# Another opening for a gated attention and SwiGLU kernel: first x tile ahead of the loads, split copies, held transposes, fixed PSUM banks

## The chip, the cores and the metric

The kernel runs on one core of a Trainium2 chip. Its time is device microseconds of one execution; lower is better. The program was executed three times before the change, with a median of 181.58 us (180.75 to 183.9). One further execution was taken with the hardware profiler; durations in this text come from it.

## The reference: what is computed

The input x has 2048 tokens of 512 features, in bf16. Two branches are computed and mixed by a gate per token:

```python
g = sigmoid((x * gate_w).sum(-1, keepdims=True))
qkv = x @ wqkv                      # 32 heads of 16
pq, pk = phi(q), phi(k)             # phi(t) = where(t>0, t+1, exp(t)) + 1e-6
kv  = einsum("bhsd,bhse->bhde", pk, v);  z = pk.sum(over tokens)
a = (pq @ kv / (pq @ z + 1e-6)) @ wo
b = (silu(x @ w1) * (x @ w3)) @ w2  # hidden size 1376
out = g * a + (1 - g) * b
```

The attention is linear: no score matrix exists, and kv is a 16 by 16 matrix per head.

## The kernel before

Tokens are cut into 16 tiles of 128 (index t) and four blocks of 512; the 512 features into four chunks of 128 (index kc). The order of the work on each engine is written out by hand: the program's order of calls is the order of instructions, and semaphore waits between engines are put in from the data that each instruction reads and writes. A PSUM tile taken from a pool waits for the last reader of the buffer that it gets.

TensorE needs x twice: token-major (xN, loaded as it is) and feature-major (xT). For the first four tiles xT is made on the chip: transpose_step (L195 to L201) transposes four 128x128 pieces of xN on TensorE into one bf16 PSUM tile, and VectorE copies all 512 columns into xT (L201). For the other twelve tiles xT comes by transposing DMAs from DRAM (L97, L100): four of 512 tokens by 128 features, then four of 1024 by 128.

All loads are issued at the top from two queues, that of SyncE (SP) and that of ScalarE (ACT). Eight DMA semaphores are used in turn: the ninth DMA of the program, the load of wq, waits for the landing of the first, and so on.

The stages on TensorE are these. The opening: ten matmuls on zeros (warm, L205), transposition of tile 0, two more warm matmuls, half of the k projection of tile 0, transposition of tile 1, the other half, transposition of tile 2, k of tile 1, transposition of tile 3, k of tiles 2 and 3. Then a loop over the tiles: the q projection of tile t, the k projection of tile t+2, and g_step, which accumulates x^T pk for tile t in four PSUM banks. phi is an Exp on ScalarE (L165) and two VectorE operations (L167, L170); each k tile is added to zacc on GpSimd (POOL, L184). After the loop come the small products for kv and its product with wo, and for each block of 512 tokens ten gate and up pairs (L251, L257), the remainder of the hidden size (rem_step), and four output steps (L378, L392).

For the prediction the order in which VectorE and ScalarE get the opening matters. Before the change all four copies of L201 stand on VectorE ahead of the first phi, because the two calls of k_phi come after the last transpose_step:

```python
transpose_step(2, psumT)
k1 = project(1, wk, "k")
transpose_step(3, psumT)
k_phi(0, k0)
k_phi(1, k1)
```

Of the kernel before, what the change touches and what calls it, by code (L numbers as in the profile page):

```python
# [16 lines left out]
def kernel(  # L17
# [17 lines left out]
    nc = tc.nc  # L35
# [12 lines left out]
    FR = F - FC * P  # L48
    F0 = FC * P
    HPC = P // Dh  # L50
    NR = 2 * FR + 1
    NPE = TPB
    ZP = 4

    x2d = A_x.flatten_outer_dims()
    out2d = out.flatten_outer_dims()
    x_r = x2d.rearrange("s (kc d) -> s kc d", d=P)
    x_t = x2d.rearrange("(t p) d -> p t d", p=P)
    wqkv_r = A_wqkv.rearrange("(kc d) n -> d kc n", d=P)
    w1_r = B_w1.rearrange("(kc d) f -> d kc f", d=P)  # L60
# [1 line left out]

    consts = ctx.enter_context(tc.tile_pool(name="consts", bufs=1))
    work = ctx.enter_context(tc.tile_pool(name="work", bufs=2))
    psum = ctx.enter_context(tc.tile_pool(name="psum", bufs=4, space=bass.MemoryType.PSUM))
    ctx.enter_context(tc.manual_schedule())

    warm = consts.tile([P, 256], BF16, name="warm")
    nc.vector.memset(warm[:], 0.0)
    ident = consts.tile([P, P], BF16, name="ident")  # L70
    make_identity(nc, ident[:])

# [8 lines left out]
    w3 = consts.tile([P, KC, F0], BF16, name="w3")  # L81
    w2 = consts.tile([P, FC + 1, D], BF16, name="w2")
    xT = consts.tile([P, KC, S], BF16, name="xT")
    dq = nc.sync
    aq = nc.scalar
    k_cols = slice(D, 2 * D)
    dq.dma_start(out=xN[:, 0, :], in_=x_t[:, 0, :])
    aq.dma_start(out=wk[:, 0, :], in_=wqkv_r[:, 0, k_cols])
    dq.dma_start(out=wk[:, 1, :], in_=wqkv_r[:, 1, k_cols])
    aq.dma_start(out=xN[:, 1, :], in_=x_t[:, 1, :])  # L90
    dq.dma_start(out=wk[:, 2, :], in_=wqkv_r[:, 2, k_cols])
    aq.dma_start(out=wk[:, 3, :], in_=wqkv_r[:, 3, k_cols])
    dq.dma_start(out=xN[:, 2, :], in_=x_t[:, 2, :])
    aq.dma_start(out=xN[:, 3, :], in_=x_t[:, 3, :])
    dq.dma_start(out=wq[:], in_=wqkv_r[:, :, 0:D])
    for kc in range(KC):
        dq.dma_start(out=xT[:, kc, TB : 2 * TB], in_=x_r[TB : 2 * TB, kc, :], transpose=True)  # L97
    dq.dma_start(out=xN[:, 4:8, :], in_=x_t[:, 4:8, :])
    for kc in range(KC):
        dq.dma_start(out=xT[:, kc, 2 * TB : S], in_=x_r[2 * TB : S, kc, :], transpose=True)  # L100
    dq.dma_start(out=xN[:, 8:12, :], in_=x_t[:, 8:12, :])
    dq.dma_start(out=xN[:, 12:16, :], in_=x_t[:, 12:16, :])
    with nc.allow_non_contiguous_dma(reason="gate column"):
        dq.dma_start(
            out=wr[:, :, 2 * FR : NR], in_=gate_w.rearrange("(kc d o) -> d kc o", d=P, o=1)
# [41 lines left out]
    def mm_tile(name):
        return psum.tile([P, D], FP32, tag="mm", name=name)


    def project(t, w, name, between=None):
        ts = slice(t * P, (t + 1) * P)
        ps = mm_tile(name + "_ps")
        for kc in range(KC):
            nc.tensor.matmul(  # L155
                ps[:], lhsT=xT[:, kc, ts], rhs=w[:, kc, :],
                start=(kc == 0), stop=(kc == KC - 1),
            )
            if kc == 1 and between is not None:
                between()  # L160
        return ps
# [25 lines left out]
                )  # L187

    def k_step(t):
        k_phi(t, project(t, wk, "k"))  # L190

    def q_step(t):
        phi(project(t, wq, "q"), pq[:, t, :], "q")

    def transpose_step(t, pool):  # L195
        ps = pool.tile([P, KC, P], BF16, tag="xTp", name="xTp")
        for kc in range(KC):
            nc.tensor.transpose(  # L198
                out=ps[:, kc, :], in_=xN[:, t, kc * P : (kc + 1) * P], identity=ident[:]
            )  # L200
        nc.vector.tensor_copy(out=xT[:, :, t * P : (t + 1) * P], in_=ps[:])  # L201

    def warm_step(ps, n):
        for _ in range(n):
            nc.tensor.matmul(  # L205
                ps[:, 0:256], lhsT=warm[:, 0:P], rhs=warm[:], start=True, stop=True
            )


    def rem_step(tb):  # L210

        hr = hrem[tb % 2]
        for half in range(2):
            ps = psum.tile([P, 2, 256], FP32, tag="mm", name="r_ps")
            for j in range(2):
                t = tb * TPB + half * 2 + j
# [28 lines left out]

    def glu_step(tb, fc):
        fs = slice(fc * P, (fc + 1) * P)
        tok = slice(tb * TB, (tb + 1) * TB)
        g_ps = mm_tile("gate_ps")
        for kc in range(KC):  # L250
            nc.tensor.matmul(  # L251
                g_ps[:], lhsT=w1[:, kc, fs], rhs=xT[:, kc, tok],
                start=(kc == 0), stop=(kc == KC - 1),
            )
        u_ps = mm_tile("up_ps")
        for kc in range(KC):
            nc.tensor.matmul(  # L257
                u_ps[:], lhsT=w3[:, kc, fs], rhs=xT[:, kc, tok],
# [40 lines left out]

    hT = {}  # L300
    hT[0] = work.tile([P, FC + 1, TB], BF16, tag="hT", name="hT")
    with tc.tile_pool(name="psumT", bufs=NPE, space=bass.MemoryType.PSUM) as psumT:
        w_ps = mm_tile("warm_ps")
        warm_step(w_ps, 10)
        transpose_step(0, psumT)
        warm_step(w_ps, 2)
        k0 = project(0, wk, "k", between=lambda: transpose_step(1, psumT))
        transpose_step(2, psumT)
        k1 = project(1, wk, "k")
        transpose_step(3, psumT)  # L310
        k_phi(0, k0)
        k_phi(1, k1)
    with tc.tile_pool(name="psumG", bufs=KC, space=bass.MemoryType.PSUM) as psumG:
        g_acc = [psumG.tile([P, D], FP32, tag="G", name=f"g_acc{kc}") for kc in range(KC)]

        def g_step(t):
            for kc in range(KC):
# [5 lines left out]
        k_step(2)
        k_step(3)
        q_step(0)
        g_step(0)
        q_step(1)
        g_step(1)
        for t in range(2, NT):
            q_step(t)  # L330
            if t + 2 < NT:
                k_step(t + 2)
            g_step(t)
        z_ps = mm_tile("z_ps")
        nc.tensor.matmul(z_ps[:], lhsT=ones[:], rhs=zaccb[:], start=True, stop=True)  # L335
        nc.vector.tensor_copy(out=zb[:], in_=z_ps[:])  # L336
        for kc in range(KC):
            if kc % 2 == 0:
                nc.vector.tensor_copy(out=Gsb[:, kc, :], in_=g_acc[kc][:])
            else:  # L340
                nc.scalar.activation(out=Gsb[:, kc, :], in_=g_acc[kc][:], func=ACT.Copy)

    psum2 = ctx.enter_context(tc.tile_pool(name="psum2", bufs=4, space=bass.MemoryType.PSUM))

    def ab_tile(name):
        return psum2.tile([P, D], FP32, tag="ab", name=name)

    def kv_step():
        kv_ps = psum2.tile([P, KC, P], FP32, tag="ab", name="kv_ps")
        for c in range(KC):  # L350
            cs = slice(c * P, (c + 1) * P)
            for kc in range(KC):
# [2 lines left out]
                    start=(kc == 0), stop=(kc == KC - 1),  # L355
                )
        nc.vector.tensor_tensor(
            out=kvT[:], in0=kv_ps[:],
            in1=bmask[:].rearrange("p h d -> p (h d)")[:, None, :].to_broadcast([P, KC, P]),
            op=ALU.mult,  # L360
        )

    def m2_step():
        for c in range(KC):
            ps = ab_tile("m2_ps")
            nc.tensor.matmul(ps[:], lhsT=kvT[:, c, :], rhs=wo[:, c, :], start=True, stop=True)  # L366
            if c % 2 == 0:
                nc.scalar.activation(out=M2[:, c, :], in_=ps[:], func=ACT.Copy)
# [3 lines left out]
    def out_step(tb, tt):  # L372
        t = tb * TPB + tt
        ts = slice(t * P, (t + 1) * P)
        tl = slice(tt * P, (tt + 1) * P)
        a_ps = ab_tile("a_ps")
        for c in range(KC):
            nc.tensor.matmul(  # L378
                a_ps[:], lhsT=pqT[:, c, ts], rhs=M2[:, c, :],
# [6 lines left out]
        w = D // pieces  # L386
        for i in range(pieces):
            cs = slice(i * w, (i + 1) * w)
            b_ps = ab_tile("b_ps")
            for fc in range(FC + 1):  # L390
                n = P if fc < FC else FR
                nc.tensor.matmul(  # L392
# [61 lines left out]
```

## Time and profile before

| what | value |
|---|---|
| time, median of three executions | 181.58 us (180.75 to 183.9) |
| time of the profiled execution | 181.63 us |
| its span, first to last instruction | 179.6 us |
| TensorE busy | 174.3 us, 97% |
| VectorE, ScalarE, GpSimd busy | 101.4, 61.8, 62.8 us |
| TensorE busy from 0 to 3.59 us, from 3.59 to 7.25, from 7.25 to 10.11 | 2.32, 3.57, 2.86 us |
| bytes moved by DMA | 14.88 MB |

The span leaves out what lies around the instructions: 181.63 - 179.6 = 2.03 us. TensorE's busy time is a sum of instruction records; matmuls overlap and their ends are modelled, so 97% says that it hardly ever stands still, not that it runs at its peak. A row of a timeline gives the start, the length, the engine and source line, the output and inputs, and in brackets how long the engine was idle ahead of it and what released it. SPq and ACTq are the queues' sequencers that issue DMAs. Landing times are counted from the issue of a DMA to its semaphore.

### The profile page before, as it was taken

To read this page: it belongs to the slowest core of one execution; us is meant where nothing else is said; L and a number is where in the kernel's file an instruction comes from. 1 tells how busy PE (TensorE), PEld (TensorE's weight loads), DVE (VectorE), ACT (ScalarE), POOL (GpSimd) and SP (SyncE) were. 2 spreads that over 40 slices of the span, in tenths; PEclk is the share of its full clock that TensorE was granted. 3 is DMA by queue.
4 is the path that set the end of the run, shared out by engine and by line. 5 is a ranking of instruction groups with operands and counts; after the bars stand their busy time and mean duration, and the time that the engine had idled before them with its cause. 6 is when DMAs were issued, how large, how long until landed. Compare 5 with 4: busy or idle time off the path is not lost.

```text
span 179.6 us, 2468 instructions
## 1 busy us (share of the span) xinstructions
PE 174.3 (97%) x860; PEld 84.4 (47%) x876; DVE 101.4 (56%) x196; ACT 61.8 (34%) x110; POOL 62.8 (35%) x105
## 2 busy tenths in 40 slices
PE   7999999999999999999999999999999999999993
PEld 4544444444445464544444454444445544444452
DVE  0398898888799672566343355644335564433222
ACT  2254454445562442222323212232321323332130
POOL 5066565676477440445400044540004432000000
PEclk9999999999999999999999999999999999999999
DMA  5989999910002112033200003520000342000011
GB/s 166 248 217 206 256 306 401 378 55 5 0 0 53 35 28 34 29 88 88 58 0 4 0 29 88 89 62 0 0 0 29 89 91 59 0 0 0 29 44 48
DMA packets 28108, 14.88 MB, mean 83 GB/s; under 512 B 19424, under 2 KB 27072, under 8 KB 28096
## 3 DMA queue, kind: packets, MB, share of 16 engines
q1 hardware_dynamic: 27520, 14.20, 30.1%
q10 hardware_dynamic: 576, 0.52, 0.8%
q8 instruction: 7, 0.11, 0.3%
q14 instruction: 5, 0.04, 0.1%
HBM read 8.42 MB, written 2.10 MB: 59 GB/s over the span
## 4 chain that ended last, share of the span: by engine, by line
PE 96%; DMA 2%; issue 1%; DVE 1%
PE b_ps L392 21%; PE gate_ps L251 19%; PE up_ps L257 19%; PE k_ps L155 8%; PE g_acc L318 8%; PE a_ps L378 8%; PE q_ps L155 8%; PE r_ps L218 3%; DMA xN<-in_A_x_dram 2%; PE xTp L198 1%; PE kv_ps L353 0%; PE m_ps L366 0%; DVE o L396 0%; DVE xT L201 0%; PE z_ps L335 0%
## 5 line engine op out<-in xcount | busy, mean ns | idle before, releaser
L263 DVE TENSOR_TENSOR hT<-up_ps,sg 128x512 bf16<-128x512 f32 x40 | 27.2, 680 | 31.0 <-PE up_ps L257 27.8
L251 PE MATMUL gate_ps<-xT,w 128*128 128x512 bf16 x158 | 41.0, 379 | 0.3
L392 PE MATMUL b_ps<-w,hT 128*128 128x512 bf16 (+3 forms) x186 | 40.6, 367 | 0.1
L257 PE MATMUL up_ps<-xT,w 128*128 128x512 bf16 x154 | 40.3, 379 | 0.2
L262 ACT ACTIVATE sg<-gate_ps 128x512 bf16<-128x512 f32 x40 | 23.9, 597 | 46.9 <-PE gate_ps L251 46.9
L285 POOL TENSOR_TENSOR pqs<-pq,rden 128x512 bf16<-128x512 bf16 x16 | 16.9, 1056 | 65.0 <-issue 60.0
L396 DVE SCALAR_TENSOR_TENSOR o<-b_ps,omg_all,aga 128x512 bf16<-128x512 f32 (+1 forms) x17 | 12.2, 720 | 28.3 <-PE b_ps L392 28.3
L392 PEld LDWEIGHTS <-hT 128*128 128x128 bf16 (+1 forms) x187 | 18.3, 98 | 19.9
L184 POOL TENSOR_TENSOR zacc<-zacc,pk 128x128 f32<-128x128 f32 x56 | 23.1, 444 | 11.5 <-DVE pk L170 11.5
L257 PEld LDWEIGHTS <-w 128*128 128x128 bf16 x160 | 15.7, 98 | 18.9
L251 PEld LDWEIGHTS <-w 128*128 128x128 bf16 x160 | 15.6, 98 | 18.5
L383 ACT ACTIVATE aga<-a_ps,g_all 128x512 f32<-128x512 f32 x16 | 11.0, 687 | 28.9 <-PE a_ps L378 28.9
L155 PEld LDWEIGHTS <-xT 128*128 128x128 bf16 x128 | 12.5, 100 | 14.7 <-DVE xT L201 0.6
L270 POOL TENSOR_TENSOR pr<-pq,zb 128x512 f32<-128x512 bf16 x16 | 18.4, 1156 | 1.7 <-DVE zb L336 1.7
L155 PE MATMUL k_ps<-wk,xT 128*128 128x512 bf16 x62 | 17.1, 396 | 0.2
L318 PE MATMUL g_acc<-pk,xN 128*128 128x512 bf16 x63 | 16.4, 379 | 0.1
L378 PE MATMUL a_ps<-M,pqT 128*128 128x512 bf16 x61 | 16.3, 378 | 0.2
L155 PE MATMUL q_ps<-wq,xT 128*128 128x512 bf16 x63 | 16.2, 379 | 0.0
L165 ACT ACTIVATE eq<-q_ps 128x512 bf16<-128x512 f32 x16 | 9.6, 597 | 17.2 <-PE q_ps L155 16.1
L165 ACT ACTIVATE ek<-k_ps 128x512 bf16<-128x512 f32 x16 | 9.6, 597 | 7.7 <-PE k_ps L155 7.5
L170 DVE SCALAR_TENSOR_TENSOR pk<-k_ps,emk 128x512 bf16<-128x512 f32 x16 | 11.1, 692 | 1.6
L170 DVE SCALAR_TENSOR_TENSOR pq<-q_ps,emq 128x512 bf16<-128x512 f32 x16 | 11.1, 692 | 0.5
(47 smaller groups left out, 94.7 us busy)
## 6 DMA issues: line engine op xcount, KB each, us to landing
w<-in_B_w_dram SPq DMA_DIRECT2D x3, 1280.0 KB, 8.5
out_dram<-o SPq DMA_DIRECT2D x15, 128.0 KB, 1.9
xN<-in_A_x_dram SPq DMA_DIRECT2D x3, 512.0 KB, 6.1
wq<-in_A_wqkv_dram SPq DMA_DIRECT2D x1, 512.0 KB, 4.7
wv<-in_A_wqkv_dram SPq DMA_DIRECT2D x1, 512.0 KB, 9.0
wo<-in_A_wo_dram SPq DMA_DIRECT2D x1, 512.0 KB, 9.5
wk<-in_A_wqkv_dram ACTq DMA_DIRECT2D x2, 128.0 KB, 3.4
xN<-in_A_x_dram SPq DMA_DIRECT2D x2, 128.0 KB, 3.3
```

Of the source, the lines that this page charges most:

```text
L155: nc.tensor.matmul(ps[:], lhsT=xT[:, kc, ts], rhs=w[:, kc, :], start=(kc == 0), stop=(kc == KC - 1),)
L165: nc.scalar.activation(out=e[:], in_=ps[:], func=ACT.Exp)
L170: nc.vector.scalar_tensor_tensor(out=dst, in0=ps[:], scalar=0.0, in1=em[:], op0=ALU.max, op1=ALU.add)
L184: nc.gpsimd.tensor_tensor(out=(zaccb if t == NT - 1 else zacc)[:, cs], in0=zacc[:, cs], in1=pk[t][:, cs], op=ALU.add,)
L251: nc.tensor.matmul(g_ps[:], lhsT=w1[:, kc, fs], rhs=xT[:, kc, tok], start=(kc == 0), stop=(kc == KC - 1),)
L257: nc.tensor.matmul(u_ps[:], lhsT=w3[:, kc, fs], rhs=xT[:, kc, tok], start=(kc == 0), stop=(kc == KC - 1),)
L262: nc.scalar.activation(out=sg[:], in_=g_ps[:], func=ACT.Silu)
L263: nc.vector.tensor_tensor(out=hT[tb][:, fc, :], in0=u_ps[:], in1=sg[:], op=ALU.mult)
L270: nc.gpsimd.tensor_tensor(out=pr[t][:], in0=pq[:, t, :], in1=zb[:], op=ALU.mult)
L318: nc.tensor.matmul(g_acc[kc][:], lhsT=xN[:, t, kc * P : (kc + 1) * P], rhs=pk[t][:], start=(t == 0), stop=(t == NT - 1),)
L378: nc.tensor.matmul(a_ps[:], lhsT=pqT[:, c, ts], rhs=M2[:, c, :], start=(c == 0), stop=(c == KC - 1),)
L392: nc.tensor.matmul(b_ps[:, 0:w], lhsT=hT[tb][:n, fc, tl], rhs=w2[:n, fc, cs], start=(fc == 0), stop=(fc == FC),)
```

## The change

Six things differ; the arithmetic of everything after the opening is the same, in the same order on TensorE.

1. **Loads.** SP issues x tile 0, wk chunks 0 and 2, x tiles 2 and 3, then wq in two halves. ACT first runs a one-element Exp (which brings the load of its function table with it) and then issues wk chunks 1 and 3 and x tile 1. Before, ACT issued wk 0, x tile 1, wk 3 and x tile 3 before any other work, and SP x tile 0, wk 1, wk 2, x tile 2 and wq in one piece.
2. **Warm matmuls** read a constant of ones that exists before the program's first barrier, in place of a tile of zeros written by VectorE. Three stand after tile 0's transposition in place of two.
3. **Transposes of tiles 0 to 3** are plain matmuls with the identity into two fp32 banks, two pieces each; VectorE copies one half (256 columns), ScalarE the other.
4. **The order of the copies and phi**: phi of tile 0 is called before the transposition of tile 3, and phi of tile 1 after it.
5. **Transposing DMAs**: twelve, one per tile of 128 tokens by 512 features. GpSimd writes one column of xT from the first half of wq; the first transposing DMA overwrites it and so waits for that half.
6. **PSUM**: eight fixed banks that are used in turn (0 to 3 for transposes, the g sums, kv, M2 and the output; 4 to 7 for projections, gate, up and remainder), in place of pools that are opened and closed.

```diff
-    warm = consts.tile([P, 256], BF16, name="warm")
-    nc.vector.memset(warm[:], 0.0)
+    warm = nc.const_aps.tensor(1.0, [P, 256], BF16)
...
-    dq.dma_start(out=xN[:, 0, :], in_=x_t[:, 0, :])
-    aq.dma_start(out=wk[:, 0, :], in_=wqkv_r[:, 0, k_cols])
-    dq.dma_start(out=wk[:, 1, :], in_=wqkv_r[:, 1, k_cols])
-    aq.dma_start(out=xN[:, 1, :], in_=x_t[:, 1, :])
-    dq.dma_start(out=wk[:, 2, :], in_=wqkv_r[:, 2, k_cols])
-    aq.dma_start(out=wk[:, 3, :], in_=wqkv_r[:, 3, k_cols])
-    dq.dma_start(out=xN[:, 2, :], in_=x_t[:, 2, :])
-    aq.dma_start(out=xN[:, 3, :], in_=x_t[:, 3, :])
-    dq.dma_start(out=wq[:], in_=wqkv_r[:, :, 0:D])
-    for kc in range(KC):
-        dq.dma_start(out=xT[:, kc, TB : 2 * TB], in_=x_r[TB : 2 * TB, kc, :], transpose=True)
-    dq.dma_start(out=xN[:, 4:8, :], in_=x_t[:, 4:8, :])
-    for kc in range(KC):
-        dq.dma_start(out=xT[:, kc, 2 * TB : S], in_=x_r[2 * TB : S, kc, :], transpose=True)
-    dq.dma_start(out=xN[:, 8:12, :], in_=x_t[:, 8:12, :])
-    dq.dma_start(out=xN[:, 12:16, :], in_=x_t[:, 12:16, :])
+    def load_xT(t):
+        ts = slice(t * P, (t + 1) * P)
+        dq.dma_start(out=xT[:, :, ts], in_=x2d[ts, :], transpose=True)
...
+    load_xN(dq, 0, 1)
+    nc.scalar.activation(out=act_pre[:], in_=warm[:, 0:1], func=ACT.Exp)
+    load_wk(dq, 0)
+    load_wk(aq, 1)
+    load_wk(dq, 2)
+    load_wk(aq, 3)
+    load_xN(aq, 1, 2)
+    load_xN(dq, 2, 3)
+    load_xN(dq, 3, 4)
+    for h in range(2):
+        hs = slice(2 * h, 2 * h + 2)
+        dq.dma_start(out=wq[:, hs, :], in_=wqkv_r[:, hs, 0:D])
+
+    nc.gpsimd.tensor_copy(out=xT[:, 0, TB : TB + 1], in_=wq[:, 1, 0:1])
+    for t in range(TPB, NT):
+        load_xT(t)
+        if t in (5, 7, 11):
+            i = {5: 4, 7: 8, 11: 12}[t]
+            load_xN(dq, i, i + 4)
...
+    bank = [psum.tile([P, D], FP32, name=f"bank{i}") for i in range(8)]
+    turn = {"mm": 0, "ab": 0}
+
+    def mm_tile():
+        turn["mm"] += 1
+        return bank[4 + (turn["mm"] - 1) % 4]
+
+    def ab_tile():
+        turn["ab"] += 1
+        return bank[(turn["ab"] - 1) % 4]
...
-        warm_step(w_ps, 10)
-        transpose_step(0, psumT)
-        warm_step(w_ps, 2)
-        k0 = project(0, wk, "k", between=lambda: transpose_step(1, psumT))
-        transpose_step(2, psumT)
-        k1 = project(1, wk, "k")
-        transpose_step(3, psumT)
-        k_phi(0, k0)
-        k_phi(1, k1)
+    def transpose_step(t, lo, hi):
+
+        ts = slice(t * P, (t + 1) * P)
+        for ps, k0 in ((lo, 0), (hi, 2)):
+            for kc in (k0, k0 + 1):
                 nc.tensor.matmul(
+                    ps[:, (kc - k0) * P : (kc - k0 + 1) * P],
+                    lhsT=xN[:, t, kc * P : (kc + 1) * P], rhs=ident[:],
+                    start=True, stop=True,
                 )
+        half = [p[:, 0 : 2 * P].rearrange("p (kc q) -> p kc q", q=P) for p in (lo, hi)]
+        nc.vector.tensor_copy(out=xT[:, 0:2, ts], in_=half[0])
+        nc.scalar.activation(out=xT[:, 2:4, ts], in_=half[1], func=ACT.Copy)
+
+    warm_step(10)
+    transpose_step(0, bank[0], bank[1])
+    warm_step(3)
+    k0 = project(0, wk, between=lambda: transpose_step(1, bank[0], bank[1]))
+    transpose_step(2, bank[2], bank[3])
+    k_phi(0, k0)
+    k1 = project(1, wk)
+    transpose_step(3, bank[0], bank[1])
+    k_phi(1, k1)
+    k_step(2)
+    k_step(3)
```

More of the change, by code (lines that the diff above doesn't have):

```diff
@@ L50 @@
     HPC = P // Dh
+    ZP = 4
     NR = 2 * FR + 1
-    NPE = TPB
-    ZP = 4
     x2d = A_x.flatten_outer_dims()
     out2d = out.flatten_outer_dims()
-    x_r = x2d.rearrange("s (kc d) -> s kc d", d=P)
     x_t = x2d.rearrange("(t p) d -> p t d", p=P)
@@ L64 @@
     work = ctx.enter_context(tc.tile_pool(name="work", bufs=2))
-    psum = ctx.enter_context(tc.tile_pool(name="psum", bufs=4, space=bass.MemoryType.PSUM))
+    psum = ctx.enter_context(tc.tile_pool(name="psum", bufs=1, space=bass.MemoryType.PSUM))
     ctx.enter_context(tc.manual_schedule())
-    warm = consts.tile([P, 256], BF16, name="warm")
-    nc.vector.memset(warm[:], 0.0)
+    warm = nc.const_aps.tensor(1.0, [P, 256], BF16)
     ident = consts.tile([P, P], BF16, name="ident")
@@ L83 @@
     xT = consts.tile([P, KC, S], BF16, name="xT")
+    act_pre = consts.tile([P, 1], BF16, name="act_pre")
     dq = nc.sync
@@ L86, with load_xN, load_wk @@
     k_cols = slice(D, 2 * D)
-    dq.dma_start(out=xN[:, 0, :], in_=x_t[:, 0, :])
-    aq.dma_start(out=wk[:, 0, :], in_=wqkv_r[:, 0, k_cols])
-    dq.dma_start(out=wk[:, 1, :], in_=wqkv_r[:, 1, k_cols])
-    aq.dma_start(out=xN[:, 1, :], in_=x_t[:, 1, :])
-    dq.dma_start(out=wk[:, 2, :], in_=wqkv_r[:, 2, k_cols])
-    aq.dma_start(out=wk[:, 3, :], in_=wqkv_r[:, 3, k_cols])
-    dq.dma_start(out=xN[:, 2, :], in_=x_t[:, 2, :])
-    aq.dma_start(out=xN[:, 3, :], in_=x_t[:, 3, :])
-    dq.dma_start(out=wq[:], in_=wqkv_r[:, :, 0:D])
-    for kc in range(KC):
-        dq.dma_start(out=xT[:, kc, TB : 2 * TB], in_=x_r[TB : 2 * TB, kc, :], transpose=True)
-    dq.dma_start(out=xN[:, 4:8, :], in_=x_t[:, 4:8, :])
-    for kc in range(KC):
-        dq.dma_start(out=xT[:, kc, 2 * TB : S], in_=x_r[2 * TB : S, kc, :], transpose=True)
-    dq.dma_start(out=xN[:, 8:12, :], in_=x_t[:, 8:12, :])
-    dq.dma_start(out=xN[:, 12:16, :], in_=x_t[:, 12:16, :])
+    def load_xT(t):
+        ts = slice(t * P, (t + 1) * P)
+        dq.dma_start(out=xT[:, :, ts], in_=x2d[ts, :], transpose=True)
+    def load_xN(q, t0, t1):
+        q.dma_start(out=xN[:, t0:t1, :], in_=x_t[:, t0:t1, :])
+    def load_wk(q, kc):
+        q.dma_start(out=wk[:, kc, :], in_=wqkv_r[:, kc, k_cols])
+    load_xN(dq, 0, 1)
[16 more added lines that the diff above has]
+            load_xN(dq, i, i + 4)
     with nc.allow_non_contiguous_dma(reason="gate column"):
@@ L145, with project @@
     th_all = consts.tile([P, NT], FP32, name="th_all")
[L147 to L153, printed above, removed]
+    bank = [psum.tile([P, D], FP32, name=f"bank{i}") for i in range(8)]
[6 more added lines that the diff above has]
+        return bank[(turn["ab"] - 1) % 4]
+    def project(t, w, between=None):
+        ps = mm_tile()
         for kc in range(KC):
             nc.tensor.matmul(
-                ps[:], lhsT=xT[:, kc, ts], rhs=w[:, kc, :],
+                ps[:], lhsT=xT[:, kc, t * P : (t + 1) * P], rhs=w[:, kc, :],
                 start=(kc == 0), stop=(kc == KC - 1),
@@ L189, in k_step, with g_step @@
     def k_step(t):
-        k_phi(t, project(t, wk, "k"))
+        k_phi(t, project(t, wk))
     def q_step(t):
-        phi(project(t, wq, "q"), pq[:, t, :], "q")
-    def transpose_step(t, pool):
-        ps = pool.tile([P, KC, P], BF16, tag="xTp", name="xTp")
+        phi(project(t, wq), pq[:, t, :], "q")
+    def g_step(t):
         for kc in range(KC):
[L198 to L204, printed above, removed]
             nc.tensor.matmul(
-                ps[:, 0:256], lhsT=warm[:, 0:P], rhs=warm[:], start=True, stop=True
+                bank[kc][:], lhsT=xN[:, t, kc * P : (kc + 1) * P], rhs=pk[t][:],
+                start=(t == 0), stop=(t == NT - 1),
             )
@@ L213, in rem_step @@
         for half in range(2):
-            ps = psum.tile([P, 2, 256], FP32, tag="mm", name="r_ps")
+            ps = mm_tile()[:].rearrange("p (j n) -> p j n", j=2)
             for j in range(2):
@@ L248, in glu_step @@
         tok = slice(tb * TB, (tb + 1) * TB)
-        g_ps = mm_tile("gate_ps")
+        g_ps = mm_tile()
         for kc in range(KC):
@@ L254, in glu_step @@
             )
-        u_ps = mm_tile("up_ps")
+        u_ps = mm_tile()
         for kc in range(KC):
@@ L301 @@
     hT[0] = work.tile([P, FC + 1, TB], BF16, tag="hT", name="hT")
-    with tc.tile_pool(name="psumT", bufs=NPE, space=bass.MemoryType.PSUM) as psumT:
-        w_ps = mm_tile("warm_ps")
-        warm_step(w_ps, 10)
-        transpose_step(0, psumT)
-        warm_step(w_ps, 2)
-        k0 = project(0, wk, "k", between=lambda: transpose_step(1, psumT))
-        transpose_step(2, psumT)
-        k1 = project(1, wk, "k")
-        transpose_step(3, psumT)
-        k_phi(0, k0)
-        k_phi(1, k1)
@@ L313, with warm_step @@
[L313 to L317, printed above, removed]
+    def warm_step(n):
+        for _ in range(n):
+            nc.tensor.matmul(
+                bank[3][:, 0:256], lhsT=warm[:, 0:P], rhs=warm, start=True, stop=True
+            )
+    def transpose_step(t, lo, hi):
+        ts = slice(t * P, (t + 1) * P)
+        for ps, k0 in ((lo, 0), (hi, 2)):
+            for kc in (k0, k0 + 1):
@@ L318, in g_step @@
                 nc.tensor.matmul(
-                    g_acc[kc][:], lhsT=xN[:, t, kc * P : (kc + 1) * P], rhs=pk[t][:],
-                    start=(t == 0), stop=(t == NT - 1),
-                )
[L323 to L346, printed above, removed]
+                    ps[:, (kc - k0) * P : (kc - k0 + 1) * P],
@@ new lines @@
+    transpose_step(2, bank[2], bank[3])
[5 more added lines that the diff above has]
+    k_step(3)
+    q_step(0)
+    g_step(0)
+    q_step(1)
+    g_step(1)
+    for t in range(2, NT):
+        q_step(t)
+        if t + 2 < NT:
+            k_step(t + 2)
+        g_step(t)
+    z_ps = mm_tile()
+    nc.tensor.matmul(z_ps[:], lhsT=ones[:], rhs=zaccb[:], start=True, stop=True)
+    nc.vector.tensor_copy(out=zb[:], in_=z_ps[:])
@@ L348, in kv_step @@
+    for kc in range(KC):
+        if kc % 2 == 0:
+            nc.vector.tensor_copy(out=Gsb[:, kc, :], in_=bank[kc][:])
+        else:
+            nc.scalar.activation(out=Gsb[:, kc, :], in_=bank[kc][:], func=ACT.Copy)
     def kv_step():
-        kv_ps = psum2.tile([P, KC, P], FP32, tag="ab", name="kv_ps")
+        kv_ps = ab_tile()[:].rearrange("p (c q) -> p c q", q=P)
         for c in range(KC):
@@ L357, in kv_step @@
         nc.vector.tensor_tensor(
-            out=kvT[:], in0=kv_ps[:],
+            out=kvT[:], in0=kv_ps,
             in1=bmask[:].rearrange("p h d -> p (h d)")[:, None, :].to_broadcast([P, KC, P]),
@@ L364, in m2_step @@
         for c in range(KC):
-            ps = ab_tile("m2_ps")
+            ps = ab_tile()
             nc.tensor.matmul(ps[:], lhsT=kvT[:, c, :], rhs=wo[:, c, :], start=True, stop=True)
@@ L375, in out_step @@
         tl = slice(tt * P, (tt + 1) * P)
-        a_ps = ab_tile("a_ps")
+        a_ps = ab_tile()
         for c in range(KC):
@@ L388, in out_step @@
             cs = slice(i * w, (i + 1) * w)
-            b_ps = ab_tile("b_ps")
+            b_ps = ab_tile()
             for fc in range(FC + 1):
```

## The prediction, made before the changed kernel ran

> **What bounds the kernel now.** I read the page's totals and its chain of waits first.
>
> ```profile
> span 179.6 us, 2468 instructions
> PE 174.3 (97%) x860; PEld 84.4 (47%) x876; DVE 101.4 (56%) x196; ACT 61.8 (34%) x110; POOL 62.8 (35%) x105
> ...
> PE 96%; DMA 2%; issue 1%; DVE 1%
> ```
>
> The chain that ended last lies 96% on TensorE, and the 2% of DMA is one transfer: x tile 0. From the opening on TensorE does not stand still, so an edit counts by how much earlier or later it lets the stream of matmuls run. Next I read the chain for the first microseconds (start, length, what).
>
> ```profile
> 0.80 2.74 DMA xN<-in_A_x_dram
> ...
> 4.71 1.03 PE k_ps L155 x2
> 5.75 0.43 PE xTp L198 x4
> 6.17 0.85 PE k_ps L155 x2
> 7.03 0.43 PE xTp L198 x4
> 7.45 0.87 PE k_ps L155 x4
> 8.32 0.22 PE xTp L198 x4
> 8.55 1.73 PE k_ps L155 x8
> ```
>
> Two k matmuls take 0.85 us at 6.17, four take 0.87 from 7.45: TensorE runs at half pace until about 7.3 us, although its clock column is full throughout. By matmul starts in the timeline the second transposition begins at 5.54, the third at 6.82, k of tile 1 at 7.25, k of tile 2 at 8.38 and k of tile 3 at 8.38 + 0.865 = 9.24. From there the stream is unbroken, so the start of **k of tile 3** after the change, against 9.24, is nearly the whole answer. The timeline shows what feeds it.
>
> ```profile
> 2.70 1.28 ACT L165 ACT_TABLE_LOAD   x1 [2.70 <-issue]
> ...
> 8.36 0.60 ACT L165 ACTIVATE ek<-k_ps 128x512 bf16<-128x512 f32 x1 [0.70 <-PE k_ps L155]
> 8.59 0.42 DVE L201 COPY xT<-xTp 128x512 bf16<-128x512 bf16 x1 [0.67 <-PE xTp L198]
> 8.93 0.28 DVE L167 TENSOR_SCALAR emk<-ek 128x512 bf16<-128x512 bf16 x1
> 9.25 0.69 DVE L170 SCALAR_TENSOR_TENSOR pk<-k_ps,emk 128x512 bf16<-128x512 f32 x1
> ```
>
> Now the copy for tile 3 (8.59 to 9.01) is ahead of all phi work on VectorE, and 0.2 us early for its user.
>
> **Part 1: the copies.** These rows price them:
>
> ```profile
> L339 DVE CAST Gsb<-g_acc 128x512 bf16<-128x512 f32 x2 | 1.3, 681 | 0.0
> ...
> L396 DVE SCALAR_TENSOR_TENSOR o<-b_ps,omg_all,aga 128x512 bf16<-128x512 f32 x15 | 11.3, 751 | 26.4 <-PE b_ps L392 26.4
> L396 DVE SCALAR_TENSOR_TENSOR o<-b_ps,omg_all,aga 128x256 bf16<-128x256 f32 x2 | 1.0, 484 | 2.0 <-PE b_ps L392 2.0
> ```
>
> On VectorE, 256 fewer fp32 columns save 751 - 484 = 267 ns, so half a tile costs about 681 - 267 = 414 ns: no less than the 425 ns of the whole bf16 tile before. On ScalarE 512 columns take 597 ns (L262) and 192 take 331 (L224), 0.83 ns each, so 256 take about 384. Halving saves only that VectorE may start after two of four pieces, about 0.2 us at half pace.
>
> **Part 2: the order on VectorE.** phi of tile 0 now stands ahead of tile 3's copy, and tile 2's ScalarE copy ahead of tile 0's Exp. Call X the start of tile 2's transposition. Its last piece is out at X + 0.67 (6.82 to 7.49 now). Then: ScalarE copy 0.38; Exp of tile 0 0.60 less 0.11 of overlap (two L341 copies of 598 take 1.08) is X + 1.54; gap 0.03 and L167 at 0.28 is X + 1.85; gap 0.04 and L170 at 0.69 is X + 2.58; the copy starts 0.08 before that ends (as 9.86 against 9.94) and takes 0.41, X + 2.91; 0.06 to TensorE (4.65 to 4.71) makes **k of tile 3 start at X + 2.97**. Now it starts at 6.82 + 2.42. The added wait is 2.97 - 2.42 = 0.55 us. If GpSimd works beside it, L167 takes 0.56 in place of 0.28 (the emq rows at 12.63 and 13.84): 0.83. GpSimd's fills are delayed into just this stretch (Part 4), so I take 0.70. Queued behind the copy are the remaining phi steps, no later than now, since tile 1's Exp ran only to 8.96. Bounds: 0, if k of tile 1 is still at half pace (TensorE then needs longer than the chain), and 0.9 if full pace begins before X.
>
> **Part 3: the loads.** Eight loads of 128 KB share the engines; now they land 2.7 to 4.0 us after issue, x tile 0 at 3.54 and x tile 1 at 4.4. Afterwards x tile 1 is third on ACT's queue, a place whose load (wk 3, issued at 1.73) lands at 5.6 now. The second transposition then starts at about 5.65 against 5.54: +0.11, and X moves with it. Lower bound: ready when TensorE is. Warm matmuls no longer wait for the zeros (that wait ends at 1.12; the queues start at 0.80 to 0.90), so ten of them end 0.2 us earlier; if x tile 0, first and alone, lands 1.9 us after issue as an output store does, tile 0's transposition starts at 3.0, its copy ends at about 3.9, a third warm matmul ends at 4.05, two k matmuls end at 4.9: -0.64. Upper bound: ACT's DMAs wait for the table load (1.28) and the Exp (0.17 by the 128x2 row). Three issues of 0.45 then start near 2.3, x tile 1's at 3.2, and it lands by the rows at hand 1.9 to 4.0 later, 5.1 to 7.2: at most +1.66. The table row shows the engine waiting for its sequencer's last DMA issue; the reverse is not in the trace.
>
> [...]
>
> [...]
>
> **Part 4: what hides.** wq's first half waits for x tile 0 (3.54) and lands 3.3 to 4.7 later, 6.9 to 8.3; q needs it at 10.1. The first transposing DMA follows by 8.4, takes 1.2 to issue (1.204 to 1.260 for L97; pqT's, of the very shape, 1.188 to 2.402) and lands 2.4 to 4.9 after issue: 13.3 at worst, against k of tile 4 at 14.59. Each further tile costs 1.2, with 0.58 for each of three x loads, against the 2.59 that the loop takes per tile, so the cover grows. SP reaches w1 at 8.4 + 12 x 1.2 + 1.7 + 1.5 for wr = 26.0 instead of 20.8; w1 lands by 34.5, gate needs it at 48.3. GpSimd's wait holds its fills (2.1 us) to 10.5 at worst; zacc starts at 10.0 now and takes 1.63 of each 2.59, so 0.5 is made up in one tile. The fixed banks rotate as the pools did, four and four, and every wait of a projection is for the same phi. Cost of all this: 0.
>
> **Sum:** 181.63 + 0.11 + 0.70 = 182.4 us; its own range, 181.7 to 183.0, comes from Part 2's 0 to 0.9 and part of Part 3's. The profiled 181.63 stands 0.05 above the median of 181.58, which I neglect.
>
> **Rivals.** *The loads win* (0.25): x tile 1 is there at 4.9, X is 6.18, k of tile 3 starts at 9.15 by the chain, or at 8.9 if the copy comes in time: 181.3 to 181.5. For it: 432 KB had moved before x tile 0 was told landed, over three times its size. Against it: its gain is eaten by the wait of Part 2. *ACT's queue is held* (0.17): x tile 1 at 6.2 to 7.2 gives +0.66 to +1.66, and with Part 2 183.0 to 184.0; if TensorE's idling there also put off full pace, +0.4 more. The change would then not even have its first tile profit. *The held transposes come too late* (0.04), the case beyond 2%: place, k of each tile from 4 on; point, an issue of over 2.5 us each (8.4 + 12c + 1.7 + landing 2.4 passes 42.9, k of tile 15). At 3.0 us it is 48.5, 5.6 late: 187. The rows of 1.19 to 1.30 speak against it; the one at 2.402 still stays under.
>
> **How the numbers follow.** Forecast 0.54, the three rivals 0.25, 0.17 and 0.04. The range 181.2 to 183.5 holds the forecast, the first rival and half of the second. About 2%, 3.6 us, is what a measurement of this kernel tells from no change; only the last rival passes it, and I leave 0.02 for something missed on the fast side: faster 0.02, same 0.93, slower 0.05.
>
> **What would show it.** In the changed profile: tile 3's VectorE copy stands after the first pk operation, and TensorE has a gap of 0.5 to 0.8 us ahead of k of tile 3, put down to that copy. ACT's first DMA issue is at about 0.9 (rival: 2.3). Transposing DMAs start at 7 to 8.5, 1.2 apart, and no k matmul from tile 4 on waits for them. From 10 us on the two traces run parallel. I am wrong if that gap is missing, if the second transposition waits past 6 us, or if a stall appears after 14 us.

## The result, and the profile after

The changed kernel takes 182.15 us (median of 20 executions, 181.15 to 184.59) against 181.26 for the kernel before beside it. The ratio is **1.0047, interval 1.0028 to 1.0066**: by that ratio 0.85 us slower, well inside the 2% and clear of zero. The prediction said 182.4, 0.8 above the profiled execution of before.

The totals and the chain by engine of the changed kernel's page:

```profile
span 179.4 us, 2503 instructions
PE 174.5 (97%) x877; PEld 83.9 (47%) x877; DVE 101.5 (57%) x195; ACT 63.4 (35%) x115; POOL 63.0 (35%) x106
...
PE 94%; DMA 2%; DVE 1%; ACT 1%; ACTq 0%; issue 0%
```

ScalarE has taken over 1.6 us of work and has come into the chain with a per cent; TensorE's share of the chain has fallen from 96 to 94%. But this span is 0.2 us *shorter* than before's, in a kernel that is slower. The profile fell on the fastest of the 20 executions, and in it TensorE's full pace came early: the trace's clock record has it from 4.8 us, before's from 7.3 (the page's clock column, full throughout, doesn't show this; the starts of the k matmuls do, 0.43 us apart up to 4.83 and 0.216 after it). One profile against one profile would have given the wrong sign here; the gaps within each trace are what can be compared. From the chain of waits of the changed kernel in its first 14 us (start, length, what):

```profile
1.76 3.93 DMA xN<-in_A_x_dram
5.69 0.04 issue
5.74 0.40 PE bank L325 x4
6.13 0.43 PE bank L174 x2
6.56 0.24 PE bank L325 x4
6.80 0.02 issue
6.83 0.39 ACT xT L332
7.21 0.50 ACT ek L184
7.71 0.02 issue
7.73 0.30 DVE emk L186
8.04 0.02 issue
8.06 0.69 DVE pk L189
8.75 0.34 DVE xT L331
9.09 0.05 issue
9.14 1.90 PE bank L174 x8
```

Where before's chain ran on TensorE from 4.71 us on, it now leaves TensorE twice. First it waits for x tile 1, third on ACT's queue, to land at 5.69. Then, from the end of tile 2's transposition, it runs through ScalarE's copy, tile 0's Exp, two VectorE operations and the copy of tile 3. The timeline has TensorE's idle time for both (in brackets), and between them k of tile 2, whose four matmuls occupy 0.865 us (half of the 1.73 us that eight take in before's chain):

```profile
5.74 0.40 PE L325 MATMUL bank<-ident,xN 128*128 128x128 bf16 x4 [0.52 <-DMA xN<-in_A_x_dram]
...
7.71 1.03 PE L174 MATMUL bank<-wk,xT 128*128 128x512 bf16 x4
...
9.14 1.04 PE L174 MATMUL bank<-wk,xT 128*128 128x512 bf16 x4 [0.40 <-DVE xT L331]
```

k of tile 3 could have started at 7.71 + 0.865 = 8.57 and started at 9.14: a hole of 0.57 us. (The bracket counts from the modelled end of the last matmul, hence 0.40.) The hole for x tile 1 is 0.52 us by its bracket, and some 0.2 us more if it too is counted by starts.

After that the traces run parallel. In all fourteen profiles the span less the start of q of tile 0 is 169.4 to 169.6 us, whatever was changed, so that start is the whole of each kernel's time within 0.2 us:

| kernel | ratio to before (interval) | full pace from, us | q of tile 0 starts, us | span, us |
|---|---|---|---|---|
| before | 1 | 7.3 | 10.11 | 179.6 |
| after | 1.0047 (1.0028 to 1.0066) | 4.8 | 10.01 | 179.4 |
| after_again | 1.0058 (1.0028 to 1.0088) | 5.5 | 10.50 | 179.9 |
| e1_order | 1.0045 (1.0014 to 1.0075) | 5.0 | 11.12 | 180.6 |
| e2_x1first | 1.0008 (0.9983 to 1.0033) | 4.5 | 9.38 | 178.8 |
| e3_both | 1.0023 (1.0000 to 1.0046) | 5.4 | 9.55 | 179.0 |
| e4_nohold | 1.0032 (1.0002 to 1.0061) | 6.1 | 10.15 | 179.6 |
| b1_order | 0.9975 (0.9948 to 1.0003) | 5.8 | 10.05 | 179.6 |
| b2_split | 1.0016 (0.9985 to 1.0048) | 7.3 | 11.16 | 180.7 |
| f1_expfirst | 0.9993 (0.9962 to 1.0024) | 6.7 | 9.75 | 179.2 |
| f2_expfirst_x1 | 0.9964 (0.9938 to 0.9990) | 9.9 | 11.79 | 181.2 |
| f2_again | 0.9958 (0.9943 to 0.9973) | 5.8 | 9.54 | 179.0 |
| f3_expfirst_loads | 0.9994 (0.9981 to 1.0007) | 6.4 | 10.09 | 179.5 |
| c1_warm | 1.0027 (0.9999 to 1.0054) | 5.1 | 9.79 | 179.3 |

The ratios come from 6 to 12 executions each, of the kernel before 29 to 35 (20 and 20 for *after*); the last three columns from one profiled execution. Executions more than 1.5% above the fastest of their kernel are left out of the ratios, among them the profiled one of f2_expfirst_x1. The names are those of the experiments below.

### The profile page after: what moved, and what is told of

Read it like the earlier page. It is cut to its first block, busy times and chain, and to the rows that moved or that the text cites. A ratio compares the mean times of both kernels' runs of the same rounds, so it can differ in the third digit from the quotient of the medians.

```text
span 179.4 us, 2503 instructions
## 1 busy us (share of the span) xinstructions
PE 174.5 (97%) x877; PEld 83.9 (47%) x877; DVE 101.5 (57%) x195; ACT 63.4 (35%) x115; POOL 63.0 (35%) x106
## 4 chain that ended last, share of the span: by engine, by line
PE 94%; DMA 2%; DVE 1%; ACT 1%; ACTq 0%; issue 0%
PE bank L407 21%; PE bank L263 19%; PE bank L269 19%; PE bank L174 14%; PE bank L393 8%; PE bank L216 8%; PE bank L230 3%; DMA xN<-in_A_x_dram 2%; PE bank L368 0%; PE bank L381 0%; DVE pk L189 0%; PE bank L325 0%; ACT ek L184 0%; DVE o L411 0%; ACTq L94 0%; ACT L97 0%
## 5 line engine op out<-in xcount | busy, mean ns | idle before, releaser
L275 DVE TENSOR_TENSOR hT<-bank,sg 128x512 bf16<-128x512 f32 x40 | 27.2, 681 | 30.9 <-PE bank L269 30.9
L269 PE MATMUL bank<-xT,w 128*128 128x512 bf16 x160 | 41.1, 379 | 0.0
L263 PE MATMUL bank<-xT,w 128*128 128x512 bf16 x160 | 41.1, 379 | 0.0
L407 PE MATMUL bank<-w,hT 128*128 128x512 bf16 (+3 forms) x187 | 40.7, 367 | 0.0
L274 ACT ACTIVATE sg<-bank 128x512 bf16<-128x512 f32 x40 | 23.9, 598 | 46.9 <-PE bank L263 46.9
L411 DVE SCALAR_TENSOR_TENSOR o<-bank,omg_all,aga 128x512 bf16<-128x512 f32 (+1 forms) x17 | 12.2, 720 | 28.4 <-PE bank L407 28.4
L174 PE MATMUL bank<-wk,xT 128*128 128x512 bf16 x64 | 16.8, 383 | 0.4 <-DVE xT L331 0.4
L174 PE MATMUL bank<-wq,xT 128*128 128x512 bf16 x64 | 16.4, 379 | 0.0
L216 PE MATMUL bank<-pk,xN 128*128 128x512 bf16 x64 | 16.4, 379 | 0.0
L393 PE MATMUL bank<-M,pqT 128*128 128x512 bf16 x64 | 16.4, 378 | 0.0
L189 DVE SCALAR_TENSOR_TENSOR pk<-bank,emk 128x512 bf16<-128x512 f32 x16 | 11.1, 692 | 1.6
```

Source lines behind the costliest of these rows:

```text
L174: nc.tensor.matmul(ps[:], lhsT=xT[:, kc, t * P : (t + 1) * P], rhs=w[:, kc, :], start=(kc == 0), stop=(kc == KC - 1),)
L189: nc.vector.scalar_tensor_tensor(out=dst, in0=ps[:], scalar=0.0, in1=em[:], op0=ALU.max, op1=ALU.add)
L216: nc.tensor.matmul(bank[kc][:], lhsT=xN[:, t, kc * P : (kc + 1) * P], rhs=pk[t][:], start=(t == 0), stop=(t == NT - 1),)
L263: nc.tensor.matmul(g_ps[:], lhsT=w1[:, kc, fs], rhs=xT[:, kc, tok], start=(kc == 0), stop=(kc == KC - 1),)
L269: nc.tensor.matmul(u_ps[:], lhsT=w3[:, kc, fs], rhs=xT[:, kc, tok], start=(kc == 0), stop=(kc == KC - 1),)
L274: nc.scalar.activation(out=sg[:], in_=g_ps[:], func=ACT.Silu)
```

## The experiments

Theory W: the wait is made by the order on VectorE, where tile 3's copy stands behind phi of tile 0. Theory L: x tile 1's later place in the loads costs. Theory C: nothing in the queues, only a later full pace. A further theory, S, came out of the first runs: ScalarE's copies hold up tile 0's Exp.

### e1_order: phi moved back behind the copies

```diff
-    k_phi(0, k0)
     k1 = project(1, wk)
     transpose_step(3, bank[0], bank[1])
+    k_phi(0, k0)
     k_phi(1, k1)
```

> The changed kernel, with the two phi calls of tiles 0 and 1 moved back behind the transposition of tile 3. Theory W (k of tile 3 waits for a VectorE copy that stands behind phi of tile 0): the gap ahead of k of tile 3, 0.56 us in the changed kernel's profile, goes to under 0.1; ratio to the kernel before falls from 1.0047 to about 1.0017 (0.56 / 181.3 = 0.0031 less). Theory L (the late landing of x tile 1 is what costs): ratio stays at 1.004 to 1.005. Theory C (the clock's full pace comes later in the changed kernel, on the mean): ratio stays too, and the gap goes without effect.

The hole ahead of k of tile 3 went, as W expects: eight k matmuls run through from 8.69. The ratio stayed, 1.0045. The chain of waits of this kernel shows why:

```profile
8.63 0.24 PE bank L325 x4
8.87 0.02 issue
8.89 0.38 ACT xT L332
9.28 0.50 ACT ek L184
9.77 0.02 issue
9.80 0.56 DVE emk L186
10.36 0.02 issue
10.38 0.70 DVE pk L189
11.08 0.04 issue
11.12 1.02 PE bank L174 x4
```

The wait moved one step on, to q of tile 0 at 11.12: q needs the PSUM bank that tile 0's pk operation frees, and now all four ScalarE copies stand ahead of tile 0's Exp. k of tile 3 started at 8.69 + 0.865 = 9.55, so q could have followed at 10.42 and lost 0.70 us. W saw one of two symptoms. This execution also had x tile 1 landing only at 6.67.

### e2_x1first and e3_both: x tile 1 first on ACT's queue

```diff
-    load_wk(aq, 1)
+    load_xN(aq, 1, 2)
     load_wk(dq, 2)
+    load_wk(aq, 1)
     load_wk(aq, 3)
-    load_xN(aq, 1, 2)
```

> The changed kernel, with x tile 1 issued first on ACT's queue, ahead of wk chunks 1 and 3. Theory L: x tile 1 lands near 4.4 us instead of 5.69, TensorE's 0.52 us gap ahead of the second transposition goes, all later steps move by that much, and the ratio to the kernel before falls from 1.0047 to about 1.002. Theory W: the gap ahead of k of tile 3 stays at about 0.5 us, since the chain that feeds it starts at tile 2's transposition and moves with it. Theory C: ratio stays.

Three of TensorE's rows in e2_x1first:

```profile
4.61 0.59 PE L174 MATMUL bank<-wk,xT 128*128 128x512 bf16 x2 [0.32 <-DMA wk<-in_A_wqkv_dram]
5.04 0.39 PE L325 MATMUL bank<-ident,xN 128*128 128x128 bf16 x4
...
8.50 1.04 PE L174 MATMUL bank<-wk,xT 128*128 128x512 bf16 x4 [0.41 <-DVE xT L331]
```

The second transposition started at 5.04 and waited for no x. TensorE waited 0.32 us for a chunk of wk instead, and the hole ahead of k of tile 3 stayed (0.41 in the bracket), as L with S or W has it. Ratio 1.0008, in line with L.

> The changed kernel with both edits: phi of tiles 0 and 1 behind the transposition of tile 3, x tile 1 first on ACT's queue. If W and L each hold, the gains add: 1.0047 - 0.0031 - 0.0029 gives a ratio of about 0.999, that is 181.0 to 181.2 us, at or below the kernel before. If only one holds, 1.002; if neither, 1.0047.

Ratio 1.0023, not 0.999: L's part shows against e1_order (1.0045), though their intervals overlap; W's doesn't add, since the wait for tile 0's pk operation stands ahead of q (0.37 in the bracket). L is left, together with something that W names only in part. C was not tested by these runs.

### e4_nohold: transposing DMAs not held

```diff
-    nc.gpsimd.tensor_copy(out=xT[:, 0, TB : TB + 1], in_=wq[:, 1, 0:1])
```

> The changed kernel without the GpSimd write from wq into xT, so that the transposing DMAs follow wq's issue at once, from about 4.2 us in place of 7.5. Forecast theory (holding them is covered): no k matmul waits for a transposing DMA in either, ratio stays at 1.004 to 1.005. Rival (the hold keeps the engines free for wk, x and wq): x tiles 2 and 3 and wq land up to 1 us later, and the ratio rises by up to 0.003. Rival (the hold costs, by GpSimd's late fills beside VectorE): the 0.56 us gap shrinks by 0.2 and the ratio falls by 0.001.

The transposing DMAs began at 5.4 us in place of 7.5. The two holes were the same (0.42 and 0.40 in the brackets), no k matmul from tile 4 on waited for xT, and 1.0032 can't be told from 1.0047. The hold is covered, as predicted.

### b2_split and b1_order: one edit alone on the kernel before

b2_split halves the copies over the two engines and leaves all else. b1_order moves phi of tile 0 ahead of tile 3's transposition and leaves all copies on VectorE.

```diff
# b2_split
-        nc.vector.tensor_copy(out=xT[:, :, t * P : (t + 1) * P], in_=ps[:])
+        nc.vector.tensor_copy(out=xT[:, 0:2, t * P : (t + 1) * P], in_=ps[:, 0:2, :])
+        nc.scalar.activation(out=xT[:, 2:4, t * P : (t + 1) * P], in_=ps[:, 2:4, :], func=ACT.Copy)
# b1_order
+        k_phi(0, k0)
         k1 = project(1, wk, "k")
         transpose_step(3, psumT)
-        k_phi(0, k0)
         k_phi(1, k1)
```

> The kernel before, with its four copies of xT halved over VectorE and ScalarE and nothing else changed (still bf16 transposes, phi of tiles 0 and 1 after all copies). Theory S (the ScalarE copies are what costs: tile 0's Exp queues behind them, and q of tile 0 needs the PSUM bank that this phi frees): Exp of tile 0 moves from 7.06 us to about 8.9, its pk operation ends near 10.5 instead of 9.94, and TensorE waits 0.4 to 0.6 us ahead of q of tile 0; ratio 1.002 to 1.003. Theory W (the order on VectorE is what costs): no gap, ratio 1.000.

> The kernel before, with phi of tile 0 called ahead of tile 3's transposition and nothing else changed (whole copies on VectorE alone). Theory W: the copy of tile 3 stands behind tile 0's pk operation, gap of 0.3 to 0.6 us ahead of k of tile 3, ratio 1.002 to 1.003. Theory S: ScalarE does Exp of tile 0 at once, as nothing stands ahead of it there; the copy of tile 3 then ends within 0.1 us of its need at half pace, and at most 0.35 late if full pace comes before tile 2's transposition; ratio 1.000 to 1.002.

The timeline of b2_split, ScalarE's and VectorE's rows and then TensorE's:

```profile
9.19 0.38 ACT L202 ACTIVATE xT<-xTp 128x256 bf16<-128x256 bf16 x1 [0.70 <-DVE xT L201]
9.47 2.06 ACT L165 ACTIVATE ek<-k_ps 128x512 bf16<-128x512 f32 x4
...
10.42 0.69 DVE L170 SCALAR_TENSOR_TENSOR pk<-k_ps,emk 128x512 bf16<-128x512 f32 x1
...
11.16 1.02 PE L155 MATMUL q_ps<-wq,xT 128*128 128x512 bf16 x4 [0.61 <-DVE pk L170]
```

Four Exps stand in a row behind the last copy, and q of tile 0 waits (0.61 us in the bracket; 0.77 by 8.66 + 8 x 0.216 = 10.39), as S says and W denies. (Everything stands later here than S forecast, since TensorE had waited 0.51 us for a chunk of wk at 6.63.) The same place in b1_order, which has the order that W blames:

```profile
6.99 0.60 ACT L165 ACTIVATE ek<-k_ps 128x512 bf16<-128x512 f32 x1 [3.01 <-PE k_ps L155]
...
8.10 0.69 DVE L170 SCALAR_TENSOR_TENSOR pk<-k_ps,emk 128x512 bf16<-128x512 f32 x1
8.71 0.41 DVE L201 COPY xT<-xTp 128x512 bf16<-128x512 bf16 x1
...
8.33 1.89 PE L155 MATMUL k_ps<-wk,xT 128*128 128x512 bf16 x8
10.05 1.03 PE L155 MATMUL q_ps<-wq,xT 128*128 128x512 bf16 x4
```

Tile 3's copy stands behind the pk operation, ends at 9.12, and k of tile 3 (8.33 + 0.865 = 9.20) doesn't wait, with less than 0.1 us to spare. With ScalarE free, tile 0's Exp had run at 6.99, so the VectorE order cost nothing here. At 0.9975 b1_order is, if anything, quicker than either theory said, but its interval includes 1. b2_split's ratio, 1.0016, is in S's direction, and its interval includes 1 too; the holes decide, not the ratios.

### f1_expfirst, f2_expfirst_x1 and f2_again: Exp ahead of the copies

```diff
+    e0 = phi_exp(k0, "k")
     transpose_step(2, bank[2], bank[3])
-    k_phi(0, k0)
+    em0 = phi_min(e0, "k")
     k1 = project(1, wk)
+    e1 = phi_exp(k1, "k")
     transpose_step(3, bank[0], bank[1])
-    k_phi(1, k1)
+    k_phi(0, k0, em0)
+    k_phi(1, k1, phi_min(e1, "k"))
```

Here phi is cut in its parts: phi_exp is the Exp on ScalarE, phi_min the first VectorE operation; k_phi then does the rest. f2 adds the load order of e2_x1first.

> The changed kernel with Exp of tile 0 ahead of tile 2's copy and Exp of tile 1 ahead of tile 3's on ScalarE, and on VectorE the order copy 2, min of tile 0, copy 3, pk of tile 0. Theory S: both gaps go, the one ahead of k of tile 3 (0.56 us) and the one that came up ahead of q of tile 0 when phi was only moved back; k of tile 3 starts 2.2 us after tile 2's transposition instead of 2.74; ratio 1.0047 - 0.003 = 1.0015 to 1.002, the rest being x tile 1's landing. If ScalarE's queue is not the cause, a gap of 0.4 us or more remains and the ratio stays at 1.0045.

Two of ScalarE's rows of f1_expfirst, and then TensorE's:

```profile
6.91 0.60 ACT L184 ACTIVATE ek<-bank 128x512 bf16<-128x512 f32 x1 [0.44 <-PE bank L174]
7.41 0.38 ACT L340 ACTIVATE xT<-bank 128x256 bf16<-128x256 f32 x1
...
6.70 0.40 PE L333 MATMUL bank<-ident,xN 128*128 128x128 bf16 x4
6.93 1.03 PE L174 MATMUL bank<-wk,xT 128*128 128x512 bf16 x4
7.80 0.39 PE L333 MATMUL bank<-ident,xN 128*128 128x128 bf16 x4
8.02 1.89 PE L174 MATMUL bank<-wk,xT 128*128 128x512 bf16 x8
9.75 1.03 PE L174 MATMUL bank<-wq,xT 128*128 128x512 bf16 x4
```

No bracket from tile 2's transposition to q: k of tile 3 starts at 8.02 + 0.865 = 8.89, 2.19 after it, where the changed kernel took 2.74. Ratio 0.9993, better than the 1.0015 expected, which its interval includes; in this profile x tile 1 landed early and wasn't waited for. The edit also puts tile 0's pk operation behind the copy of tile 3, so by itself it doesn't part S from W; that rests on b2_split and b1_order.

> The same, with x tile 1 also first on ACT's queue. If theory S and theory L both hold, TensorE's only gaps after its first matmul are those for x tile 0 and wk 0 or 1 (up to 0.3 us each); 181.0 us, ratio 0.997 to 0.999: faster than both kernels. If L was noise, as f1, 1.0015 to 1.002.

> Exp first on ScalarE and x tile 1 first on ACT's queue, once more, since the first profile of it fell into an execution in which wk came late and the clock's full pace at 9.9 us. Theory S with L: ratio 0.996 to 0.998 again; in the profile no gap ahead of k of tile 3 or q of tile 0, and the second transposition waits for nothing; at most 0.3 us for a chunk of wk.

Ratios 0.9964 and 0.9958, both intervals below 1: with the two costs out, the changed opening beats the kernel before, by about 0.7 us. In the profile of f2_again the only waits after tile 0 are for a chunk of wk, 0.20 in the bracket. In f2_expfirst_x1's profile a chunk of wk came at 6.8, and full pace only at 9.9.

### f3_expfirst_loads, c1_warm and after_again

f3 puts the eight first loads back on before's queues in before's order, on top of f1. c1 is the kernel before with the warm matmuls on the constant. after_again is the changed kernel beside f2_again.

```diff
# f3_expfirst_loads, the loads
-    load_wk(dq, 0)
-    load_wk(aq, 1)
+    load_wk(aq, 0)
+    load_wk(dq, 1)
+    load_xN(aq, 1, 2)
     load_wk(dq, 2)
     load_wk(aq, 3)
-    load_xN(aq, 1, 2)
     load_xN(dq, 2, 3)
-    load_xN(dq, 3, 4)
+    load_xN(aq, 3, 4)
# c1_warm
-    warm = consts.tile([P, 256], BF16, name="warm")
-    nc.vector.memset(warm[:], 0.0)
+    warm = nc.const_aps.tensor(1.0, [P, 256], BF16)
...
```

> Exp first on ScalarE, and the eight loads of x tiles 0 to 3 and wk on the queues and in the order of the kernel before (ACT: wk 0, x 1, wk 3, x 3), still behind the table load and the Exp on ACT. Theory L: same as f2_again within 0.002, since x tile 1 is second on ACT in place of third; ratio 0.996 to 0.999. If the order of wk matters as much as that of x, it is faster than f2_again by about 0.3 us, the wait for wk in its neighbours' profiles.

A miss: 0.9994, against 0.9958 for f2_again beside it. ScalarE's part of its timeline shows one reason:

```profile
4.10 0.33 ACTq L91 DMA_DIRECT2D xN<-in_A_x_dram  x1
4.49 0.38 ACT L340 ACTIVATE xT<-bank 128x256 bf16<-128x256 f32 x1 [2.18 <-DMA wk<-in_A_wqkv_dram]
```

With the loads in this order the fourth DMA on ACT's queue, x tile 3, got a semaphore that a load of wk still held. It was issued at 4.10 and not at about 2.2, and the transposition of tile 3 waited for it (0.30 in the bracket), which is part of the 0.6 us between the two medians. Tile 0's ScalarE copy, queued behind it, started at 4.49 where f2_again has 3.99, but nothing on TensorE waited for that copy. (In the kernel before, too, the load of wq waits for a chunk of wk, 1.1 us, and not for x tile 0.)

> The kernel before, with the ten warm matmuls on the constant of ones (no wait for VectorE's zeros) and nothing else changed. Theory: TensorE starts at 0.84 us instead of 1.12, but tile 0's transposition waits for x tile 0 either way, so only the clock can gain; ratio 0.998 to 1.001. If the earlier start is what makes the variants with Exp first faster than the kernel before, ratio 0.996 to 0.998 here too.

TensorE started at 0.84, and the ratio is 1.0027 (0.9999 to 1.0054): the earlier warm-up alone gains nothing. The ratio lies above the 1.001 expected, and no run says why.

> The changed kernel once more, beside the next three on one chip. Theory S with L: ratio 1.003 to 1.006; in its profile x tile 1 lands 3.6 to 4.9 us after its issue at 1.76, TensorE waits for it, and a gap of about 0.55 us stands ahead of k of tile 3. If x tile 1 lands before 4.9 us this time, only the second gap stands.

Ratio 1.0058, with a median 1.4 us above f2_again's, and the same two holes: 0.85 us for x tile 1, which landed 4.41 after its issue, and k of tile 3 at 9.63 where 8.19 + 0.865 = 9.06 was possible, 0.57.

## Why the prediction was right

The time, the sign and the size came out; point by point, one reason behind them did not. That the sum, 0.81, meets the 0.85 us measured is in part luck: 0.70 was too much, 0.11 too little, and a gain was left out.

- **Part 1, the copies.** Estimated 414 and 384 ns; measured 423 (L331) and 385 (L332). The half tile costs VectorE what the whole one did before (425), and ScalarE's share comes on top.
- **Part 2, the wait ahead of k of tile 3.** Forecast: X + 2.97, of which 0.55 us is loss, or 0.83 with GpSimd beside it. Measured: X + 2.74 and a loss of 0.57 us, and 0.57 again in after_again. Full pace came ahead of X (4.8 against 6.40), for which I had set 0.9; at full pace the chain got shorter by 0.23, as the last piece of the transposition was out at X + 0.43 and not X + 0.67, and TensorE's own way to k of tile 3 shrank alike, from 2.42 to 2.17. I took 0.70 because GpSimd's fills would double the first L186; that one took 0.29 (the second took 0.71). The chain was named link by link, ScalarE's copy among them, but its **cause was put down to the order on VectorE, and that failed**: b1_order has that order and no wait, e1_order undoes it and loses 0.70 us one step later. The link that matters is ScalarE's copy ahead of tile 0's Exp: b2_split has the late Exp without that order and waits, and with the Exp first (f1_expfirst) the wait is gone. The order on VectorE decides only which user of the late Exp waits, k of tile 3 or q of tile 0.
- **Part 3, the loads.** Landing of x tile 1 forecast at 5.6, measured 5.69, with ACT's queue not held. The +0.11 was mis-sized all the same: it compared with 5.54, before's start at half pace, while TensorE was ready 0.52 us ahead of the landing. With x tile 1 third on ACT's queue TensorE waited 0.52, 0.85, 1.32, 0.42 and 0 us (after, after_again, e1_order, e4_nohold, f1_expfirst), 0.62 on the mean of the brackets. Three pairs differ in this place alone: e2 against after, e3 against e1 and f2 against f1 give 0.0039, 0.0022 and 0.0029, 0.4 to 0.7 us; in the last two the intervals overlap, and the first two kernels did not run beside each other. The sign of being wrong that I named, a second transposition past 6 us, came up in after_again (6.21), with the DMA issued at 1.75 all the same. My reading of one landing as *the* landing was the weak point: for the same place it was 3.4 to 4.9 us.
- **What I left out of the sum is a gain**: the costs of 0.57 and 0.4 to 0.7 less the 0.85 measured leave a gain of 0.1 to 0.4 us, and with both costs taken away f2 is 0.7 us faster than the kernel before. Some of it is visible: tile 0 is transposed at 3.33 us on the mean of the ten profiles of kernels built on the changed one, at 3.56 in the four built on the kernel before, and behind the start of q the ten take 169.4 us, the four 169.5. The kernel before has a wait of its own as well: b1_order, b2_split and c1_warm wait 0.31, 0.51 and 0.40 us for wk. The rest may be an earlier full pace (theory C's question, the other way round), but one profile each can't settle that, and c1_warm, with it at 5.1 us, is not faster. This stays open.
- **ACT's queue is held**, a rival, fell. Its DMAs are issued at 0.86 us, during the table load:

```profile
0.80 1.28 ACT L97 ACT_TABLE_LOAD   x1 [0.80 <-PEq L453]
0.86 0.86 ACTq L94 DMA_DIRECT2D wk<-in_A_wqkv_dram  x2
1.76 0.45 ACTq L91 DMA_DIRECT2D xN<-in_A_x_dram  x1
```

The queue ran ahead of its engine: two DMAs are issued from 0.86 to 1.72 and the third at 1.76, while the table load runs from 0.80 to 2.08. So x tile 0 was never alone: it landed at about 3.3, not at the 2.7 that an output store's 1.9 us would give. In the +0.11 the queue's not being held was my assumption; no row of the kernel before shows it.

- **The held transposes** cost nothing: the first is issued at 7.50 (forecast 7 to 8.5), the median issue takes 1.264 us (forecast 1.2), none is waited for, and e4_nohold is no faster.
- **When full pace comes.** At half pace the k matmuls start 0.43 us apart, at full pace 0.216. Full pace began between 4.5 and 7.3 us in thirteen of the fourteen profiles, 3.7 to 6.2 after the first matmul, and at 9.9, 9.1 after it, in that of f2_expfirst_x1; in that execution TensorE had stood still 0.9 us for wk. The 2.8 us between 4.5 and 7.3 are worth up to 1.4 us at half pace (an estimate from the two distances, for a TensorE that works throughout), more than the 0.85 us of the change. What sets the moment was not shown. Two terms in the rivals of the prediction suppose something about it that no run shows: the 8.9 of the first is 9.24 less half of 0.64, as if full pace came at 7.3 however early the work starts, and the 0.4 of the second has it later when TensorE idles. The runs show the spread above instead, with 4.8 in the changed kernel; in after_again it came at 5.5, within TensorE's wait for x tile 1 (up to 6.21).

## What to carry to other kernels

Work moved onto an idle engine is not free if that engine's next instruction is on the critical chain: look at what queues behind it (here a 0.39 us copy ahead of an Exp whose result frees a PSUM bank), and place the urgent instruction first. When a wait is taken away, look for the next user of the same late result before counting the gain. Where the opening of a kernel varies by more than the edit from one execution to the next, compare holes within a trace and many executions, never two spans.

## What the runs showed of the hardware that was not expected

- The reverse of the queue running ahead was seen too: in f3_expfirst_loads a DMA on ACT's queue that waited for a semaphore held up the ScalarE copy behind it (the DMA was issued at 4.10 instead of about 2.2, the copy started at 4.49 where f2_again has 3.99).
- A 128 KB load in the same place of the same queue landed 3.4, 3.9, 3.9, 4.4 and 4.9 us after issue in five executions (f1_expfirst, after, e4_nohold, after_again, e1_order). In all fourteen profiles the first four loads issued have landed by 4.8 us, and the next four only between 4.9 and 7.5 (x tile 3 of f3_expfirst_loads, issued at 4.10, apart). In the changed kernel x tile 1 is one of the late four; with x tile 1 first, two chunks of wk are among them, and TensorE waits for wk (0.20 us in f2_again, 0.90 in f2_expfirst_x1).
- The same TENSOR_SCALAR on 128x512 bf16 took 0.28 us in f2_again from 10.49 on, where GpSimd idles from 10.31 to 10.73, and 1.00 us from 8.84 on, while GpSimd ran two fills of hrem (0.98 us from 8.71).
